# Spectral filter and segmented attention on one core: part of the spectrum's butterflies on GpSimd, and the third bf16 part of q and k by a subtraction

## The chip, the cores and the metric

The kernel runs on one core of a Trainium2 chip. A core has five engines that work side by side, each on its own queue of instructions in a fixed order: TensorE (PE, matrix products), VectorE (DVE), ScalarE (ACT), GpSimd (POOL) and SyncE (SP, which here only issues transfers). They wait for each other by semaphores. The metric is the time of one execution on the device in microseconds (us); lower is better.

## The reference

Two independent computations, side by side in the output. A is a segmented attention with a memory (32 heads of width 18, four segments of 512 rows), B multiplies the 2-D Fourier spectrum of x by a weight.

```python
# A: x (2048 x 576); N = 4 segments of L = 512, H = 32 heads, Dh = 18
q, k, v = x @ wq, x @ wk, x @ wv              # split into heads and segments
for s in range(4):
    logits = einsum("bhqd,bhkd->bhqk", qs, ks) * scale + causal_mask
    a_dot = softmax(logits) @ vs
    a_mem = (phi(qs) @ M) / (phi(qs) . z + 1e-6)      # phi(t) = t+1 if t>0 else exp(t)
    o = g * a_mem + (1 - g) * a_dot                   # g = sigmoid(beta) per head
    M, z = M + phi(ks)^T @ vs, z + sum(phi(ks))
a = concat(o) @ wo
# B: x (2048 x 576)
b = irfft2(rfft2(x) * (w_r + 1j * w_i), s=(2048, 576))
out = concatenate([a, b], axis=-1)
```

## The kernel before

All engines' orders are written out by hand: the order in which the Python program emits instructions is the order of each engine's queue, and nothing reorders them. The time falls into these stages.

1. **Forward transform** (`FFT.forward`, about the first 75 us). For each of 16 units u: VectorE makes sums and differences of two halves of x (`eo`, L125) and low parts (`el`, L131, L132), TensorE multiplies by the tables of the row transform (L142), ScalarE and VectorE split the result in a high and a low part (`X`, L146, L149), TensorE does the 128-point column transform (L162) and ScalarE puts the result in `Z` (L153). `Z` holds 16 complex tiles of 128 x 290 in four by four, real and imaginary parts side by side, so that one tile is 580 elements wide. GpSimd's queue issues the loads of the coefficients `cfw` (L118, four buffers). VectorE also splits the weights wq and wk (L406).
2. **Projections** (`projections`, about 75 to 285 us): four groups g of 512 rows; in each, nine q/k units (14 products of 512 columns, L460, then splitting the result in three bf16 parts that are stored by SP) and four v units (28 products of 288 columns; GpSimd's memsets L507 and L508 fill the constant columns of the v tile, ScalarE copies the values, and the state M, z is accumulated by `pm` (L517), masked by VectorE (L525) and added by GpSimd (L529 to L533)). In the same stage x of the next group is split (L433, L439).
3. **Inverse transform** (`inverse`, about 285 to 355 us) and **attention** (to the end).

The rest of the column transform lies between the first and the third stage: `Z` needs, along its axis of sixteen, a four-point butterfly over each column of tiles (`stage1`), twiddle factors (`tws`, products by a constant on ScalarE and the additions on VectorE), for each c a second butterfly, the product by the weight W, an inverse butterfly and inverse twiddles (`middle`), and a last butterfly (`last`). A butterfly `bf` is ten VectorE instructions (L206): six of 580 elements and four of 290, from `Z` into four temporaries and back to `Z`; there are 16 of them. A weight product is four instructions (L245, L247 of 580 and L250, L252 of 290); there are 16. The tiles of W are loaded by SP (L235, three buffers), each load behind the product that frees its buffer.

These chains are generators that yield after each VectorE instruction, in one list `pace.q`. `Pace.take(f)` lets f of their instructions into the queue at that place. So `forward` takes one per unit from the eighth unit on and two per unit from the fifteenth; `projections` takes w per unit, spread over the four groups, w being 2.4 times as large for a v unit as for a q/k unit.

The splitting of q and k (`qk_unit`) goes: ScalarE writes the first bf16 part from the accumulator in PSUM (L472) and, where needed, computes phi (L475, L476); VectorE finishes phi (L478) and subtracts the first part from the accumulator (L479); ScalarE writes the second part (L483); TensorE subtracts it by a product with the negative identity `nid` (L485), and ScalarE writes the third part (L486). The accumulators are five PSUM buffers.

Of the kernel before, what the change touches and what calls it, by code (L numbers as in the profile page):

```python
# [102 lines left out]
class FFT:  # L103
# [4 lines left out]
    def forward(s,xp,cp,pp,wl,xs,consts):  # L108
# [88 lines left out]
    def bf(s,x,y,inv):  # L197

        v=s.nc.vector; tp=s.tp
        t=[tp.tile([128,2,FP],F32,name=f"t{i}",tag="t",bufs=8) for i in range(4)]  # L200
        p,m=(y[1],y[3]) if not inv else (y[3],y[1])
        for o,a,b,op in ((t[0],x[0],x[2],OP.add),(t[1],x[0],x[2],OP.subtract),(t[2],x[1],x[3],OP.add),(t[3],x[1],x[3],OP.subtract),
                         (y[0],t[0],t[2],OP.add),(y[2],t[0],t[2],OP.subtract),
                         (p[:,0],t[1][:,0],t[3][:,1],OP.add),(p[:,1],t[1][:,1],t[3][:,0],OP.subtract),
                         (m[:,0],t[1][:,0],t[3][:,1],OP.subtract),(m[:,1],t[1][:,1],t[3][:,0],OP.add)):
            v.tensor_tensor(o,a,b,op=op)  # L206
            yield
    def tws(s,L,inv):

        nc=s.nc; v=nc.vector; A=[]; L=[x for x in L if x[1]]  # L210
        if not L: return
        for i in range(len(L)+1):
            if i<len(L):
                y,e=L[i]; a=-2*np.pi*e/16*(-1 if inv else 1)
                t=[s.tp.tile([128,2,FP],F32,name=f"tw{k}",tag="t",bufs=8) for k in range(2)]
                nc.scalar.activation(t[0],y,AF.Copy,scale=float(np.cos(a)))
                nc.scalar.activation(t[1],y,AF.Copy,scale=float(np.sin(a)))
                A.append((y,t))
                if i==0: yield
            if i>0:  # L220
                y,t=A.pop(0)
                v.tensor_tensor(y[:,0],t[0][:,0],t[1][:,1],op=OP.subtract)
                yield
                v.tensor_tensor(y[:,1],t[0][:,1],t[1][:,0],op=OP.add)
                yield
    def stage1(s,b):
        x=[s.Z[:,b,a] for a in range(4)]
        yield from s.bf(x,x,False)
        yield from s.tws([(x[c],b*c) for c in (2,1,3)],False)
    def middle(s,wp):  # L230
        nc,io=s.nc,s.io; v=nc.vector
        Ws=[]
        def ld(i):
            W=wp.tile([128,2,FP],F32,name="W",bufs=3)
            nc.sync.dma_start(W,io["w"][i//4][:,i%4])  # L235
            Ws.append(W)
        for i in range(3): ld(i)
        for c in range(4):
            x=[s.Z[:,b,c] for b in range(4)]
            yield from s.bf(x,x,False)  # L240
            for d in range(4):
                W=Ws[4*c+d]
                t=s.tp.tile([128,2,FP],F32,name="wm",tag="t",bufs=8)
                t2=s.tp.tile([128,2,FP],F32,name="wm2",tag="t",bufs=8)
                v.tensor_tensor(t,x[d],W[:,0][:,None,:].to_broadcast([128,2,FP]),op=OP.mult)  # L245
                yield
                v.tensor_tensor(t2,x[d],W[:,1][:,None,:].to_broadcast([128,2,FP]),op=OP.mult)  # L247
                if 4*c+d+3<16: ld(4*c+d+3)
                yield
                v.tensor_tensor(x[d][:,0],t[:,0],t2[:,1],op=OP.subtract)  # L250
                yield
                v.tensor_tensor(x[d][:,1],t[:,1],t2[:,0],op=OP.add)  # L252
                yield
            yield from s.bf(x,x,True)
            yield from s.tws([(x[b],b*c) for b in (2,1,3)],True)
# [12 lines left out]
    def last(s):  # L268

        for b in range(4):  # L270
            x=[s.Z[:,b,c] for c in range(4)]
            yield from s.bf(x,x,True)
# [69 lines left out]
BF=mybir.dt.bfloat16  # L342
# [42 lines left out]
class ATT:  # L385
# [36 lines left out]
    def xprep(s,g,t,hp,xp,w,tag,bufs):  # L422
# [12 lines left out]
        else:  # L435
            l=s.ftp.tile([128,2,FP],F32R,name="xt",tag="t",bufs=8).rearrange("p a b -> p (a b)")[:,:512]
# [25 lines left out]
    def qk_unit(s,g,mt,tp,pp):  # L462
# [22 lines left out]
        nc.tensor.matmul(ps,s.nid,sp3[:,1],start=False,stop=True,skip_group_check=True)  # L485
        nc.scalar.copy(sp3[:,2],ps)  # L486
# [47 lines left out]
    def projections(s,xp,tp,pp,wv,pace,hook):  # L534

        live=[]
        s.nid=wv.tile([128,128],BF,name="nid"); s.nc.scalar.activation(s.nid,s.ident,AF.Copy,scale=-1.0)
# [505 lines left out]
def emit(nc,tc,io):  # L1043
    def pool(es,name,bufs=1,**kw):
        return es.enter_context(tc.tile_pool(name=name,bufs=bufs,reuse_waits="tile",**kw))
    with ExitStack() as L0:
# [9 lines left out]
        with tc.manual_schedule():  # L1056
# [5 lines left out]
            with ExitStack() as es:  # L1062
                wv=pool(Rv,"wv"); xp=pool(es,"xp"); tp=pool(es,"tp",2); fwp=pool(es,"fw",2)
                pp=es.enter_context(PP(tc,"pp",dict(pj=5,pt=1,pm=2)))
                F.pace.add(F.middle(fwp)); F.pace.add(F.last())
# [13 lines left out]
                A.projections(xp,tp,pp,wv,F.pace,hook)  # L1079
# [37 lines left out]
```

## Time and profile before

| | us |
|---|---|
| median of 3 runs | 725.89 |
| lowest, highest | 725.75, 726.9 |
| span of the profiled execution | 725.3 |
| busy time in that span: TensorE / VectorE / ScalarE / GpSimd | 693.1 / 551.2 / 455.1 / 209.4 |

The profiled execution's own time is its span and lies 0.6 us below the median of the runs. In the rows below, PE is TensorE, DVE VectorE, ACT ScalarE, POOL GpSimd, and SPq the queue of transfers on SyncE. A row of grouped instructions has the line, engine, operation, what is written and read, the shapes and the count, then busy us and mean ns of one, then the engine's idle time before them and who ended it. A row of the timeline has start and duration in us. A row by stretch has, for each engine, busy us and instructions in brackets.

### The profile page before, as it was taken

The page shows a single profiled execution, that of the slowest core. Times are in us where ns is not written, and L with a number is a line of the kernel's source. Part 1 is how long each engine was busy: PE and PEld are TensorE (multiplying, and loading weights), DVE is VectorE, ACT ScalarE, POOL GpSimd, SP SyncE. Part 2 cuts the span into 40 slices and gives each one's busy share as a digit, 9 for nine tenths or more (in the row PEclk, how much of TensorE's full clock was granted, in tenths as well). Part 3 has the DMA queues.
Part 4 walks back from the last instruction along what each step waited for, and adds up shares of the span by engine and source line. Part 5 has one row for each costly group of instructions (what it writes and reads, how often), then busy time and mean ns, then how long its engine had stood idle before and what let it go on. Part 6 is the DMA issues. An engine that isn't in the chain of part 4 may idle for free.

```text
span 725.3 us, 14481 instructions
## 1 busy us (share of the span) xinstructions
PE 693.1 (96%) x5007; PEld 498.8 (69%) x5007; DVE 551.2 (76%) x1281; ACT 455.1 (63%) x1008; POOL 209.4 (29%) x410
## 2 busy tenths in 40 slices
PE   4998999999999999999999999999899999999897
PEld 4988779879779889999844444444565445663397
DVE  6999879899799789787587878877466875667433
ACT  3665796585586574444487777767466776567531
POOL 2111000100200112565065434444142762335310
PEclk9999999999999999999999999999999999999999
DMA  9884435545363668898537656777546675441142
GB/s 339 274 261 156 136 127 183 193 168 177 124 217 131 189 206 275 208 234 224 168 102 185 173 148 146 186 165 159 141 98 172 176 172 133 111 118 41 33 144 84
DMA packets 83245, 121.06 MB, mean 167 GB/s; under 512 B 11352, under 2 KB 50630, under 8 KB 83036
## 3 DMA queue, kind: packets, MB, share of 16 engines
q1 hardware_dynamic: 76580, 104.11, 50.5%
q0 software_dynamic: 6592, 16.03, 7.8%
q8 instruction: 39, 0.64, 0.4%
q14 instruction: 34, 0.28, 0.1%
HBM read 81.78 MB, written 38.24 MB: 165 GB/s over the span
## 4 chain that ended last, share of the span: by engine, by line
PE 76%; DVE 8%; DMA 7%; ACT 5%; issue 3%; POOL 1%; SPq 0%; ACTq 0%; DVEq 0%; POOLq 0%
PE pj L460 14%; PE pv L709 9%; PE s L638 9%; PE pjv L460 8%; PE po L843 7%; PE i L296 4%; PE i L307 4%; PE s L681 3%; PE s L685 2%; PE po L872 2%; DVE eo L125 2%; PE s L690 2%; PE pn L778 2%; PE s L647 2%; PE pm L517 2%
## 5 line engine op out<-in xcount | busy, mean ns | idle before, releaser
L642 DVE CUSTOM_DVE_ANT_0 junk<-s,x 128x512 bf16<-128x512 f32 (+1 forms) x256 | 141.2, 552 | 62.3 <-PE s L638 58.6
L694 POOL TENSOR_SCALAR_AFFINE_SELECT P<-P 128x512 f32<-128x512 f32 x128 | 78.5, 645 | 82.3 <-ACT P L682 74.6
L648 DVE TENSOR_REDUCE mx<-s 128x4 f32<-128x512 f32 x128 | 87.9, 687 | 12.8 <-PE s L647 11.0
L709 PE MATMUL pv<-P,vs 128*32 128x512 f32 (+3 forms) x1024 | 88.8, 442 | 1.0 <-POOL P L694 1.0
L682 ACT ACTIVATE P<-s 128x512 f32<-128x512 f32 x128 | 76.2, 595 | 13.7 <-PE s L681 11.0
L691 ACT ACTIVATE P<-s 128x256 f32<-128x256 f32 x128 | 49.1, 384 | 52.8 <-PE s L690 52.5
L687 ACT ACTIVATE P<-s 128x512 f32<-128x512 f32 x128 | 75.7, 591 | 0.0
L638 PE MATMUL s<-Ks,Qs 108*128 108x384 bf16 (+3 forms) x256 | 69.1, 302 | 1.1 <-DVE mx L648 0.9
L460 PE MATMUL pj<-x,wqkh 128*128 128x512 f32 x162 | 56.5, 409 | 0.0
L638 PEld LDWEIGHTS <-Qs 108*128 108x128 bf16 x320 | 31.6, 99 | 31.5 <-issue 21.9
L206 DVE TENSOR_TENSOR Z<-t,t 128x290 f32<-128x290 f32 (+1 forms) x96 | 48.4, 553 | 0.1
L206 DVE TENSOR_TENSOR t<-Z 128x580 f32<-128x580 f32 x64 | 46.1, 755 | 0.0
L507 POOL MEMSET vt<- 128x32 f32 x16 | 2.3, 161 | 150.5 <-PE pm L517 123.9
L647 PE MATMUL s<-tri,idb 128*128 128x128 bf16 x256 | 43.0, 219 | 0.0
L142 PE MATMUL f<-ftab,eh 128*128 128x290 f32 (+1 forms) x160 | 30.8, 310 | 9.4 <-DMA ftab<-ftab 9.4
L296 PE MATMUL i<-civ,Y 128*128 128x256 f32 (+1 forms) x288 | 39.2, 288 | 0.2 <-POOL Y L281 0.2
L296 PEld LDWEIGHTS i<-civ,Y 128*128 128x128 f32 (+1 forms) x288 | 36.5, 181 | 1.1 <-POOL Y L281 0.4
L709 PEld LDWEIGHTS pv<-P,vs 128*32 128x32 f32 x1024 | 22.1, 108 | 21.9 <-issue 14.5
L307 PE MATMUL i<-itab,T 128*128 128x290 f32 (+1 forms) x224 | 36.3, 305 | 0.1
L460 PE MATMUL pj<-x,wqkl 128*128 128x512 f32 x90 | 35.5, 395 | 0.0
L460 PE MATMUL pj<-xh,wqkl 128*128 128x512 f32 x90 | 35.5, 395 | 0.0
L460 PE MATMUL pj<-xh,wqkh 128*128 128x512 f32 x90 | 35.5, 395 | 0.0
(201 smaller groups left out, 1809.8 us busy)
## 6 DMA issues: line engine op xcount, KB each, us to landing
qkD<-sp SPq DMA_DIRECT2D x36, 384.0 KB
Ks<-qkD SPq DMA_DIRECT2D x72, 144.0 KB
x<-qkD SPq DMA_DIRECT2D x60, 144.0 KB
Qs<-qkD SPq DMA_DIRECT2D x60, 144.0 KB
xin<-xb SPq DMA_DIRECT2D x16, 384.0 KB
cfw<-cfw POOLq DMA_DIRECT2D x16, 384.0 KB, 4.5
civ<-civ POOLq DMA_DIRECT2D x16, 384.0 KB, 7.4
vs<-vD SPq DMA_DIRECT2D x16, 330.0 KB
```

What stands on the lines that cost most here:

```text
L206: v.tensor_tensor(o,a,b,op=op)
L296: nc.tensor.matmul(p[:m,k],Y[i][:,q,c*128:c*128+m],cc[:,hl,o:o+256],start=n==0,stop=n==5)
L307: nc.tensor.matmul(p,x,t,start=n==0,stop=n==6)
L460: s.nc.tensor.matmul(out,a,b,start=i==0,stop=i==len(L)-1)
L638: nc.tensor.matmul(out,Q[:108,h,128*i:128*i+128],K[:108,h,:128*(i+1)],start=True,stop=True)
L642: nc.vector.tensor_tensor_reduce(out=junk[:,:w],in0=src,in1=s.mask[:,512-w:],scale=1.0,scalar=-3.0e38, op0=OP.add,op1=OP.max,accum_out=s.m ...
L647: nc.tensor.matmul(pa[:,o+w-128:o+w],s.idb,s.tri,start=False,stop=True,skip_group_check=True)
L648: nc.vector.tensor_reduce(out=s.mx[k][:,hh],in_=pa.rearrange("p (b c) -> p b c",c=128),axis=mybir.AxisListType.X,op=OP.max)
L682: nc.scalar.activation(P[0][:,hh],p0,AF.Exp,scale=SC)
L687: nc.scalar.activation(P[1][:,hh],p1,AF.Exp,scale=SC)
L694: nc.gpsimd.affine_select(out=x,in_=x,pattern=pat+[[1,128]],compare_op=OP.is_ge,fill=0.0,base=0,channel_multiplier=-1)
L709: nc.tensor.matmul(s.pvt[32*hh:32*hh+32,128*j:],vt[:,j,19*h:19*h+32],mv[0][:,hh,mv[1]],start=j==0,stop=j==2,skip_group_check=True)
```

## The change

- **Butterflies in place.** `bf` works in `Z` itself with two temporaries instead of four: the difference goes to a temporary, the sum over its first operand. The instructions stay ten, six of 580 and four of 290.
- **Part of the chains on GpSimd.** The engine is an argument. GpSimd gets the butterflies of the first stage for b = 0 and 1, and for c = 0 and 1 of the middle both butterflies and the weight products: 20 and 72 instructions. The twiddles stay on ScalarE and VectorE; where a GpSimd chain comes before them they are put at the head of VectorE's list. `s.part` counts finished parts: the middle begins when four are finished, the last butterflies when eight are.
- **Two lists.** `gp` is a second `Pace`. `forward` takes three of its instructions per unit, ahead of the loads of `cfw` in GpSimd's queue; VectorE's list is taken from only after the fourteenth unit. `projections` takes 72/28 of `gp` per unit and w of VectorE's list, now 3.0 times as large for v units.
- **Buffers.** VectorE's temporaries go from eight to five, GpSimd has two of its own, W has two buffers for each of the two chains instead of three in all.
- **Third part of q and k.** The product with `nid` and ScalarE's cast are replaced by one VectorE subtraction from PSUM that writes bf16. `nid` is gone.

```diff
-        s.pace=Pace(61+165+40)
+        s.pace=Pace(41+94+40); s.gp=Pace(20+72); s.part=0
...
-            if u%4==3 and u>6: s.pace.add(s.stage1((u-7)//4))
+            if u%4==3 and u>6:
+                b=(u-7)//4
+                (s.gp if b<2 else s.pace).add(s.stage1(b))
...
-            if u<14: s.pace.take(1)
+            s.gp.take(3)
...
+    def temp(s,eng,n):
+        g=eng is s.nc.gpsimd
+        return [s.tp.tile([128,2,FP],F32,name=f"{'g' if g else 't'}{i}",tag="g" if g else "t",bufs=2 if g else 5) for i in range(n)]
+    def bf(s,x,inv,eng):
+        A,B=s.temp(eng,2)
+        p,m=(x[1],x[3]) if not inv else (x[3],x[1])
+        for o,a,b,op in ((A,x[0],x[2],OP.subtract),(x[0],x[0],x[2],OP.add),(B,x[1],x[3],OP.subtract),(x[1],x[1],x[3],OP.add),
+                         (x[2],x[0],x[1],OP.subtract),(x[0],x[0],x[1],OP.add),
+                         (p[:,0],A[:,0],B[:,1],OP.add),(p[:,1],A[:,1],B[:,0],OP.subtract),
+                         (m[:,0],A[:,0],B[:,1],OP.subtract),(m[:,1],A[:,1],B[:,0],OP.add)):
+            eng.tensor_tensor(o,a,b,op=op)
+            yield
...
     def stage1(s,b):
+        tw=s.tws([(x[c],b*c) for c in (2,1,3)],False)
+        if b<2:
+            yield from s.bf(x,False,s.nc.gpsimd)
+            if b==1: s.pace.q.insert(0,s.count(tw))
+            else: s.part+=1
+        else:
+            yield from s.bf(x,False,s.nc.vector)
+            yield from s.count(tw)
+    def count(s,g):
+        yield from g
+        s.part+=1
-    def middle(s,wp):
+    def middle(s,wp,cs,eng):
+        while s.part<4: yield
...
+            W=wp.tile([128,2,FP],F32,name="Wg" if g else "W",bufs=2)
...
     def last(s):
+        while s.part<8 and s.gp.one(): pass
+        while s.part<8: yield from s.pace.q.pop(0)
...
-        nc.tensor.matmul(ps,s.nid,sp3[:,1],start=False,stop=True,skip_group_check=True)
-        nc.scalar.copy(sp3[:,2],ps)
+        nc.vector.tensor_tensor(sp3[:,2],ps,sp3[:,1],op=OP.subtract)
...
-                w=tot/(36+16*2.4)*(1.0 if i<9 else 2.4)
+                w=tot/(36+16*3.0)*(1.0 if i<9 else 3.0); gw=72/28.0
                 advance()
-                pace.take(w*.4)
+                pace.take(w*.4); gp.take(gw*.4)
                 advance()
                 next(u)
-                pace.take(w*.6)
+                pace.take(w*.6); gp.take(gw*.6)
...
-                F.pace.add(F.middle(fwp)); F.pace.add(F.last())
+                F.gp.add(F.middle(fwp,(0,1),nc.gpsimd)); F.pace.add(F.middle(fwp,(2,3),nc.vector)); F.pace.add(F.last())
```

More of the change, by code (lines that the diff above doesn't have):

```diff
@@ L214, in tws @@
                 y,e=L[i]; a=-2*np.pi*e/16*(-1 if inv else 1)
-                t=[s.tp.tile([128,2,FP],F32,name=f"tw{k}",tag="t",bufs=8) for k in range(2)]
+                t=s.temp(v,2)
                 nc.scalar.activation(t[0],y,AF.Copy,scale=float(np.cos(a)))
@@ L236, in ld @@
+    def count(s,g):
+        yield from g
+        s.part+=1
+    def middle(s,wp,cs,eng):
+        nc,io=s.nc,s.io; g=eng is nc.gpsimd
+        while s.part<4: yield
+        Ws=[]; J=[(c,d) for c in cs for d in range(4)]
+        def ld():
+            if len(Ws)==len(J): return
+            c,d=J[len(Ws)]
+            W=wp.tile([128,2,FP],F32,name="Wg" if g else "W",bufs=2)
+            nc.sync.dma_start(W,io["w"][c][:,d])
             Ws.append(W)
[L237 to L238 removed]
+        ld(); ld()
+        for n,c in enumerate(cs):
@@ L239, in middle @@
             x=[s.Z[:,b,c] for b in range(4)]
-            yield from s.bf(x,x,False)
+            yield from s.bf(x,False,eng)
             for d in range(4):
[L242 to L245, printed above, removed]
+                W=Ws[4*n+d]
+                t,t2=s.temp(eng,2)
+                eng.tensor_tensor(t,x[d],W[:,0][:,None,:].to_broadcast([128,2,FP]),op=OP.mult)
@@ L253, in middle @@
                 yield
-            yield from s.bf(x,x,True)
-            yield from s.tws([(x[b],b*c) for b in (2,1,3)],True)
+            yield from s.bf(x,True,eng)
+            tw=s.tws([(x[b],b*c) for b in (2,1,3)],True)
+            if g and c: s.pace.q.insert(0,s.count(tw))
+            elif g: s.part+=1
+            else: yield from s.count(tw)
     def inv_setup(s,cp):
@@ L533, in v_unit, with projections @@
                 nc.gpsimd.tensor_tensor(z,m[:r,:w,18],s.zst[g][:r,t,:w],op=OP.add)
-    def projections(s,xp,tp,pp,wv,pace,hook):
-        live=[]
-        s.nid=wv.tile([128,128],BF,name="nid"); s.nc.scalar.activation(s.nid,s.ident,AF.Copy,scale=-1.0)
+    def projections(s,xp,tp,pp,wv,F,hook):
+        live=[]; pace,gp=F.pace,F.gp
         lw=s.load_w("wv",576,wv,xp,288,"xl",4)
@@ L1078, in emit @@
                 q0=[]
-                A.projections(xp,tp,pp,wv,F.pace,hook)
+                A.projections(xp,tp,pp,wv,F,hook)
             Rv.close()
```

28 lines of the change are left out of this document (6 added, 22 removed).

## The prediction

> **What bounds the kernel now.** I read the page first (busy shares, chain), then busy times by stage, then the rows of VectorE and GpSimd in the stages that the change touches.
>
> ```profile
> span 725.3 us, 14481 instructions
> ...
> PE 693.1 (96%) x5007; PEld 498.8 (69%) x5007; DVE 551.2 (76%) x1281; ACT 455.1 (63%) x1008; POOL 209.4 (29%) x410
> ...
> PE 76%; DVE 8%; DMA 7%; ACT 5%; issue 3%; POOL 1%; SPq 0%; ACTq 0%; DVEq 0%; POOLq 0%
> ```
>
> TensorE is busy nearly throughout, but the shares are means over stages. By stretch (16.5 us of the forward transform, then the four groups of the projections):
>
> ```profile
> core 0: us, PE busy (x) PEld busy (x) DVE busy (x) ACT busy (x) POOL busy (x), PEclk, DMA share, GB/s
> 42.00:58.50 16.50, 15.09 (x105) 14.15 (x106) 16.25 (x29) 10.23 (x21) 2.12 (x4) 1.00 0.82 248
> 75.56:127.98 52.42, 51.22 (x289) 43.13 (x288) 44.91 (x89) 41.78 (x85) 0.35 (x4) 1.00 0.47 155
> 127.98:180.94 52.96, 52.96 (x308) 45.16 (x308) 48.11 (x89) 34.39 (x67) 3.06 (x18) 1.00 0.57 184
> 180.94:235.00 54.06, 53.50 (x308) 45.44 (x308) 45.78 (x86) 37.91 (x74) 4.30 (x18) 1.00 0.46 158
> ```
>
> In the forward transform VectorE is the bound (16.25 of 16.5 us). In the projections TensorE is, with VectorE at 85 to 91%. GpSimd is nearly idle in both, which is where the change puts its work. From about 285 us on (inverse, attention) the change touches nothing and I take it as shifted only.
>
> **Part 1: the product.** Its price on TensorE is the step between projection tiles:
>
> ```profile
> 245.56 3.26 PE pj L460 x14
> 249.04 3.26 PE pj L460 x14
> ```
> ```profile
> L485 PE MATMUL pj<-sp,nid x36: 376/389/393, 83.6 to 273.9; 128*128 128x512 bf16 x36
> ```
>
> One tile is 3.26 us and the next starts 3.48 us later: 0.22 to 0.23 us per product, so 36 x 0.23 = 8.3 us where TensorE stays the bound, about 2.05 us for each group of nine. ScalarE loses 36 casts that stood behind it. VectorE gains 36 subtractions from PSUM, which I price by the row of the same shape:
>
> ```profile
> L478 DVE SCALAR_TENSOR_TENSOR ex<-pj,ex 128x512 f32<-128x512 f32 x9 | 6.2, 689 | 5.1 <-ACT ex L476 4.9
> L479 DVE TENSOR_TENSOR pj<-pj,sp 128x512 f32<-128x512 f32 x9 | 6.2, 689 | 0.0
> L206 DVE TENSOR_TENSOR Z<-t,t 128x290 f32<-128x290 f32 x12 | 4.9, 453 | 0.0
> L206 DVE TENSOR_TENSOR Z<-t,t 128x580 f32<-128x580 f32 x6 | 4.4, 752 | 0.0
> ...
> L433 DVE TENSOR_TENSOR xl<-xst,xh 128x512 fp32r<-128x512 f32 x4 | 2.7, 684 | 0.0
> ```
> ```profile
> 46.66 1.02 DVE L125 TENSOR_TENSOR eo<-xin 128x384 f32<-128x384 f32 x2
> 47.60 0.76 DVE L149 TENSOR_TENSOR X<-f,X 128x580 fp32r<-128x580 f32 x1
> 48.27 0.75 DVE L206 TENSOR_TENSOR t<-Z 128x580 f32<-128x580 f32 x1
> 48.94 0.68 DVE L131 TENSOR_TENSOR el<-eo,eh 128x512 fp32r<-128x512 f32 x1
> 49.66 0.42 DVE L132 TENSOR_TENSOR eh<-eo,eh 33x256 fp32r<-33x256 f32 x1
> 50.11 0.76 DVE L406 TENSOR_TENSOR wqkl<-raw,wqkh 128x576 fp32r<-128x576 f32 x1
> ```
>
> Starts lie 0.08 us closer than durations (47.60 to 48.27 is 0.67 for 0.75), so a VectorE step is 0.67 us for 580 wide, 0.61 for 512, 0.37 for 290. The new subtraction adds 36 x 0.61 = 22 us to VectorE.
>
> **Part 2: what GpSimd takes.** A butterfly is 6 instructions of 580 and 4 of 290; a weight product 2 and 2. GpSimd gets 2 butterflies in the forward transform (20 instructions) and 4 butterflies with 8 products in the projections (72). For VectorE that is 6 x 5.5 + 8 x 2.08 = 50 us less. GpSimd's own rates:
>
> ```profile
> L813 POOL TENSOR_TENSOR ol<-am,oh 126x512 fp32r<-126x512 f32 x8 | 10.2, 1273 | 8.6 <-ACT oh L810 6.8 <-PE s L690 1.7
> ...
> L610 POOL TENSOR_TENSOR wol<-ob,woh 126x576 fp32r<-126x576 f32 x5 | 7.1, 1411 | 7.0 <-ACT woh L609 6.5 <-PE s L686 0.5
> ...
> L739 POOL TENSOR_TENSOR ry<-ry,rw 128x128 f32<-128x128 f32 x8 | 3.4, 429 | 23.0 <-ACT rw L738 22.9
> ```
>
> A line through 128, 512 and 576 gives 0.15 us + 2.19 ns per element: 1.42 us at 580, 0.79 at 290. 92 instructions are 105 us, twice what VectorE takes.
>
> **Do they run side by side?** The trace has a few places where both engines read two operands from SBUF:
>
> ```profile
> 700.03 0.43 POOL L739 TENSOR_TENSOR ry<-ry,rw 128x128 f32<-128x128 f32 x1 [14.48 <-ACT rw L738]
> 700.53 0.63 POOL L740 CAST rw<-ry 128x128 bf16<-128x128 f32 x1
> 701.24 0.75 POOL L741 TENSOR_TENSOR rw<-ry,rw 128x128 bf16<-128x128 f32 x1
> ```
> ```profile
> 700.13 0.88 DVE L854 TENSOR_TENSOR ux<-ux,am 126x512 f32<-126x512 f32 x1
> 700.93 0.77 DVE L859 TENSOR_TENSOR P<-ux,P 126x512 fp32r<-126x512 f32 x1
> 701.63 0.68 DVE L853 TENSOR_TENSOR ux<-ux,pb 126x512 f32<-126x512 f32 x1
> 702.34 0.69 DVE L854 TENSOR_TENSOR ux<-ux,am 126x512 f32<-126x512 f32 x1
> ```
>
> L854 takes 0.88 us behind L739 and 0.69 alone: it ends 0.55 us after L739's end, so it stood until 0.14 us before that end. L741, of L739's shape, takes 0.75 instead of 0.43: it ends 0.29 us after L859, again 0.14 before the end of the other. L740 got in between L854 and L859, so the engines take turns. L853, which reads one operand from PSUM, runs beside L741 at its usual 0.68. So a two-SBUF-operand instruction of one engine holds off the other's for its duration less 0.14 us, and only VectorE's PSUM instructions cover GpSimd. Hold times: GpSimd 1.28 (580) and 0.645 (290), VectorE 0.61 and 0.31. A butterfly on GpSimd holds 10.3 us, a product 3.85: 20.5 us in the forward transform, 71.8 in the projections.
>
> The Trainium skill (SBUF — State Buffer, Who interferes with whom) has the two engines' shared pair as a lock held for the whole instruction. By that, each of the 92 would hold 0.14 us longer, 13 us in all; the rows above show the release earlier, and I sum by the rows.
>
> **Forward transform.** One iteration on VectorE is 4.13 us, all of it taken. Without its butterfly instruction it is 3.46, with X (0.67, from PSUM) as the only cover. GpSimd is handed three instructions per iteration, 3.08 us of hold. Over 6.7 iterations VectorE then has 23.1 + 20.5 us less an overlap of at most 4.5 (X), 39.1 against 27.5 before: +11.6; without any overlap +16. If GpSimd falls behind into the last, emptier iterations, less is paid: +3. GpSimd's queue also issues the coefficient loads (cfw) behind these instructions; they are used three iterations later, so a lag of some 8 us stays hidden. I take +9.
>
> **Projections.** VectorE's pace falls to 153/84 = 1.82 instructions per q/k unit and 5.46 per v unit, 38 per group; GpSimd's middle part starts when the first stage is complete (third v unit of the first group) and runs 28 units at 2.57: 2.15 groups. In such a group VectorE's own steps are 27 PSUM instructions (16.5 us), the state products (1.2), five x splits (3.0), 38 spectrum instructions at 0.51 (19.6) and some 1.4 us of waits on its own earlier instruction, which chains in place have more often: 41.7 us. TensorE needs 54.06 - 2.05 = 52.0. GpSimd holds 33.4 x 1.0 = 33.3 us. For the group to stay at 52.0, 23.0 of these 33.3 must fall on VectorE's PSUM instructions and idle time (28 us together). Holds alone (20.1 + 33.3) give 53.4 us as the least; an overlap of half the PSUM time gives 66. I take 17 us of overlap: 58, since a q/k unit has 2 or 3 PSUM instructions in a row against one 1.28 us hold. That is +4 per group against 54.06, x 2.15 = +8.6 [-1.5 to +26]. The other 1.85 groups gain 2.05 each: -3.8. The loads of weights on SP's queue:
>
> ```profile
> SPq L235 <- DVE wm L247: 28.6, 13, 4.6
> ```
>
> They go from three buffers to two per chain, and half of them then wait for a GpSimd product, with the stores of q, k and v queued behind. I price it at 0 while the q/k tiles are three buffers deep; it costs up to this row's 4.6 us a time where that cover is used up. The ring of temporaries (8 to 5) costs nothing: a butterfly in place needs two of them instead of four.
>
> **Sum**: 725.3 (the profiled execution, 0.6 below the median) + 9 + 8.6 - 3.8 = 739.1; against the median of 725.89 that is **739.7**.
>
> **Rivals.**
> A, faster: the cover suffices. VectorE has 10.3 us idle per group plus 17.7 of PSUM work; if GpSimd fills 23 of it and lags harmlessly in the forward transform, TensorE stays the bound: 725.9 - 8.3 + 3 = 720.5 (down to 717.6 with no loss at all). Point of decision: 23 us of overlap per group. For it: GpSimd's idle; against: holds of 1.28 us are longer than two PSUM steps. Chance 0.20.
> B, worse: GpSimd's order becomes the bound.
>
> ```profile
> POOL vt L507 <- DMA vD<-vt: 16.6, 3, 8.5
> ...
> DVE mm L525 <- POOL zst L533: 2.1, 6, 0.5
> ```
>
> Memsets of v tiles wait up to 8.5 us for a store, with butterflies now queued behind; ScalarE's v copies wait for those memsets, and VectorE's state products for GpSimd's copies, behind its whole backlog. A lag of 5 to 8 us at three group ends: 739.7 + 15 to 24, about 757. Chance 0.15.
> C, the hold lasts for whole instructions under load: up to 13 us more, 750. The same page of the Trainium skill says this; chance 0.03.
> D, gains and losses cancel within 0.2% (which is what a measurement tells from no change): 0.04.
>
> Forecast (734 to 750): 0.58. With C that makes slower 0.76, same 0.04, faster 0.20. The range 720 to 758 takes in most of A and B.
>
> **What would show it.** Right: VectorE's 580-wide SBUF instructions rise from 0.75 to over 1.2 us on average beside GpSimd's, those from PSUM stay at 0.69; the forward iterations go from 4.1 to 5 us or more; TensorE is idle in the second and third group; L485 is gone. Wrong: if durations stay at 0.75 under load, or TensorE stays dense from 120 to 230 us, A holds; if GpSimd is idle behind memsets while ScalarE waits for them, B.

## The result, and the profile after

The changed kernel takes 754.3 us (median; 752.5 to 754.8) against 725.8 for the kernel before in the same rounds: ratio 1.039 [1.037, 1.041], slower by 28.5 us. The forecast was slower by 13.8 in a range of 720 to 758. The page of the changed kernel, its span, busy shares, granted clock in 40 slices, and shares of the chain that ended last:

```profile
span 752.1 us, 14427 instructions
...
PE 692.3 (92%) x4971; PEld 503.5 (67%) x4971; DVE 584.5 (78%) x1225; ACT 436.6 (58%) x971; POOL 323.0 (43%) x502
...
PEclk9988999999999999999999999999999999999999
...
PE 60%; DVE 19%; ACT 7%; issue 6%; DMA 4%; POOL 3%; SPq 0%; DVEq 0%; ACTq 0%; POOLq 0%
```

TensorE has no more work than before (692 against 693 us) and VectorE has 56 instructions fewer, yet VectorE is busy for 33 us longer: its instructions have become longer. The chain runs through VectorE for 19% of the span instead of 8. By stage, from the starts of the first projection product and the first inverse product in each trace:

| stage | before | after | difference | forecast |
|---|---|---|---|---|
| forward transform, to the first projection | 75.4 | 94.0 | +18.6 | +9 |
| projections | 208.0 | 217.7 | +9.7 | +4.8 |
| inverse and attention | 441.9 | 440.4 | -1.5 | 0 |
| span | 725.3 | 752.1 | +26.8 | +13.8 |

Stage times here and below come from one profiled execution of each kernel. How far they can be trusted shows in the seven kernels below whose forward transform is VectorE's alone: it ends between 74.6 and 76.8 us, so a difference of 1 or 2 us in a stage proves little.

The busy times by stretch: first the same seven forward iterations (from the sixth `X` to the thirteenth) in the kernel before and in the changed kernel, where GpSimd's butterflies fall into them; then the four groups of the projections in the changed kernel (52.4, 53.0, 54.1 and 48.6 us before). Columns as in the prediction.

```profile
core 0: us, PE busy (x) PEld busy (x) DVE busy (x) ACT busy (x) POOL busy (x), PEclk, DMA share, GB/s
31.40:60.84 29.44, 27.58 (x192) 25.94 (x192) 28.69 (x51) 17.88 (x35) 4.03 (x8) 1.00 0.79 242
```
```profile
31.84:78.12 46.28, 31.70 (x200) 29.98 (x199) 43.82 (x44) 17.86 (x35) 28.73 (x28) 0.85 0.53 161
94.00:142.80 48.80, 48.80 (x281) 42.65 (x280) 44.99 (x75) 33.81 (x69) 7.80 (x9) 1.00 0.54 170
142.80:204.70 61.90, 54.48 (x301) 47.42 (x300) 60.23 (x78) 31.61 (x61) 44.16 (x53) 0.94 0.47 159
204.70:265.30 60.60, 52.89 (x300) 45.91 (x300) 58.33 (x73) 30.14 (x59) 45.95 (x52) 0.97 0.42 141
265.30:311.67 46.37, 46.37 (x259) 40.67 (x259) 38.83 (x73) 25.23 (x50) 6.61 (x22) 1.00 0.73 238
```

The first group, with five of GpSimd's spectrum instructions, and the last, with none (7.8 and 6.6 us busy), got shorter, by 3.6 and 2.2 us, with TensorE busy to the last tenth. The two with GpSimd at 44 to 46 us got longer, by 8.9 and 6.5, and there VectorE has only 1.7 and 2.3 us left idle, with 73 to 78 instructions against 86 to 89 before. In the forward iterations VectorE is busy for 43.8 of 46.3 us with 44 instructions, 1.00 us each; before it was 51 in 28.7, 0.56 each.

Which instructions got longer, in the second group of the changed kernel (grouped by line and form: busy us, mean ns of one, idle before):

```profile
L210 DVE TENSOR_TENSOR Z<-Z 128x580 f32<-128x580 f32 x8 | 10.6, 1324 | 0.2
L454 DVE TENSOR_TENSOR x<-xst,x 128x512 fp32r<-128x512 f32 x4 | 6.2, 1558 | 0.0
L261 DVE TENSOR_TENSOR t<-Z,W 128x580 f32<-128x580 f32 x4 | 6.2, 1549 | 0.0
L500 DVE TENSOR_TENSOR pj<-pj,sp 128x512 f32<-128x512 f32 x9 | 6.1, 683 | 0.0
L506 DVE TENSOR_TENSOR sp<-pj,sp 128x512 bf16<-128x512 f32 x9 | 6.1, 678 | 0.0
L499 DVE SCALAR_TENSOR_TENSOR ex<-pj,ex 128x512 f32<-128x512 f32 x9 | 6.1, 677 | 0.3 <-ACT ex L497 0.3
```

The split is clean. Instructions with both operands in SBUF take 1.3 to 1.6 us instead of 0.75 (580) or 0.68 (512). Instructions that read one operand from PSUM, the new L506 among them, keep their 0.68. GpSimd pays too, though less: 1.72 us for an instruction of 580 over both groups, against 1.42 on the prediction's line.

```profile
L210 POOL TENSOR_TENSOR Z<-Z 128x580 f32<-128x580 f32 x16 | 27.4, 1715 | 0.8
```

One figure is used from here on, the **stretch**: the sum over VectorE's instructions of their duration less the short (5th per cent) duration of the same form, where that is over 0.06 us. It is worked out from all rows of VectorE's timeline. Beside it stands what VectorE was **relieved** of, at the prediction's 5.5 us per butterfly and 2.08 per weight product, and GpSimd's hold times as the prediction added them up.

| | relieved | hold | stretch |
|---|---|---|---|
| before, projections | 0 | 0 | 0.1 |
| after, forward transform | 11.0 | 20.5 | 18.7 |
| after, projections | 38.6 | 71.8 | 42.0 |

In both stages VectorE loses more by standing than it was relieved of: 60.7 us against 49.6. The holds are a little high: the prediction's line gave 0.79 us at 290, where the shortest in the changed kernel is 0.69 to 0.70, and the shortest of the weight product's 580 is 1.32. With these the holds are 19.8 and 67.5 us, and the stretch is 94 and 62% of them instead of 91 and 58%.

### The profile page after: what moved, and what is told of

It reads as the page before. It is cut to its first block, busy times and chain, and to the rows that moved or that the text cites. A ratio compares the mean times of both kernels' runs of the same rounds, so it can differ in the third digit from the quotient of the medians.

```text
span 752.1 us, 14427 instructions
## 1 busy us (share of the span) xinstructions
PE 692.3 (92%) x4971; PEld 503.5 (67%) x4971; DVE 584.5 (78%) x1225; ACT 436.6 (58%) x971; POOL 323.0 (43%) x502
## 3 DMA queue, kind: packets, MB, share of 16 engines
q1 hardware_dynamic: 76580, 104.11, 48.6%
## 4 chain that ended last, share of the span: by engine, by line
PE 60%; DVE 19%; ACT 7%; issue 6%; DMA 4%; POOL 3%; SPq 0%; DVEq 0%; ACTq 0%; POOLq 0%
PE pv L728 9%; PE s L657 9%; PE po L862 7%; PE pj L481 6%; PE pjv L481 5%; PE i L317 4%; PE i L328 4%; PE s L700 3%; DVE Z L210 2%; DVE eo L125 2%; PE s L704 2%; PE po L891 2%; DVE wqkl L427 2%; PE s L709 2%; PE s L666 2%
## 5 line engine op out<-in xcount | busy, mean ns | idle before, releaser
L710 ACT ACTIVATE P<-s 128x256 f32<-128x256 f32 x128 | 49.1, 383 | 52.9 <-PE s L709 52.5
L504 ACT CAST sp<-pj 128x512 bf16<-128x512 f32 x36 | 21.1, 585 | 57.8 <-DVE pj L500 57.8
L162 PE MATMUL c<-X,cfw 128*128 128x290 f32 x192 | 32.1, 322 | 19.6 <-ACT Z L153 19.5
L162 PEld LDWEIGHTS c<-X,cfw 128*128 128x128 f32 x192 | 28.9, 207 | 21.9 <-ACT Z L153 21.9
L210 POOL TENSOR_TENSOR Z<-Z 128x580 f32<-128x580 f32 x24 | 40.3, 1678 | 1.3
L682 POOL CAST mh<-mg 128x16 bf16<-128x16 f32 x32 | 6.2, 194 | 78.3 <-ACT mg L680 47.1
L210 DVE TENSOR_TENSOR Z<-Z 128x580 f32<-128x580 f32 x40 | 38.7, 966 | 1.0
```

The lines of the kernel that those rows point to most:

```text
L162: nc.tensor.matmul(p[:,:FP],cc[:,hl,k*128:(k+1)*128],x[i][:,q],start=n==0,stop=n==5)
L210: eng.tensor_tensor(o,a,b,op=op)
```

## The experiments

The theory: GpSimd's two-operand instructions and VectorE's from SBUF exclude each other, and what VectorE stands there is the loss. The rival: VectorE has no room for the 36 subtractions of part 1, whatever GpSimd does. Most runs below take one of them away or leave one alone. The butterflies in place and the shorter rings of buffers were not run by themselves; the memset run below has both and is the fastest of all, so the loss isn't theirs. Ratios are against the kernel before, timed in the same rounds.

### The subtractions alone

```diff
 (kernel before)
-        nc.tensor.matmul(ps,s.nid,sp3[:,1],start=False,stop=True,skip_group_check=True)
-        nc.scalar.copy(sp3[:,2],ps)
+        nc.vector.tensor_tensor(sp3[:,2],ps,sp3[:,1],op=OP.subtract)
```

> The subtraction alone: the kernel before with the product by nid and ScalarE's cast replaced by VectorE's subtraction, everything of the spectrum left on VectorE as before. Port theory (GpSimd's two-operand instructions hold off VectorE's): nothing on GpSimd, so only part 1 remains: TensorE loses 36 x 0.23 = 8.3 us, VectorE gains 5.5 us in a group of 54 us where it had 8.3 idle, so it just fits: 718 to 724 us. Rival (VectorE is already too full, and the 22 us of subtractions are a good part of the loss): 727 to 735 us.

Measured: 737.5 us, ratio 1.016 [1.013, 1.019]. Slower, above both expectations: part 1 alone costs 11.7 us. Its four groups and the beginning of the inverse transform:

```profile
75.90:127.30 51.40, 49.20 (x280) 42.52 (x279) 49.02 (x95) 37.63 (x75) 0.34 (x4) 1.00 0.48 157
127.30:179.80 52.50, 51.41 (x300) 44.59 (x299) 50.24 (x92) 27.76 (x54) 2.89 (x16) 1.00 0.57 185
179.80:237.80 58.00, 52.10 (x301) 44.63 (x300) 54.33 (x103) 35.38 (x68) 4.47 (x20) 1.00 0.44 148
237.80:284.20 46.40, 46.40 (x260) 40.68 (x259) 41.86 (x78) 23.46 (x47) 6.61 (x22) 1.00 0.72 237
284.20:300.00 15.80, 9.35 (x58) 8.74 (x57) 13.49 (x21) 5.52 (x14) 5.68 (x8) 0.80 0.41 122
```

VectorE goes to 94 to 96% in the first three groups. They save 1.0 and 0.5 us instead of 2.05 each, and the third loses 3.9. The projections take as long as before (208.3 against 208.0 us), but less of the spectrum is done by then: 24 of VectorE's spectrum instructions start behind the first inverse product, against 17 before, and the inverse transform takes 82.7 us against 74.0. They meet a second thing there, GpSimd's subtractions for Y:

```profile
288.67 2.37 POOL L281 TENSOR_TENSOR Y<-Z,Y 128x512 fp32r<-128x512 f32 x2 [1.98 <-ACT Y L280]
290.54 4.36 DVE L206 TENSOR_TENSOR Z<-t,t 128x580 f32<-128x580 f32 x5
295.60 4.18 PE L296 MATMUL i<-civ,Y 128*128 128x256 f32 x18 [5.46 <-issue]
```

Five instructions of 580 take 4.36 us in which they would take some 3.4 alone (0.67 each), and TensorE stands for 5.46 us before its next products (the profile names no releaser, so that VectorE's lateness is what it waits for is not shown). So the rival is real: VectorE's room is gone with 22 us more.

### GpSimd's part alone

```diff
 (changed kernel)
-        nc.vector.tensor_tensor(sp3[:,2],ps,sp3[:,1],op=OP.subtract)
+        nc.tensor.matmul(ps,s.nid,sp3[:,1],start=False,stop=True,skip_group_check=True)
+        nc.scalar.copy(sp3[:,2],ps)
```

> The GpSimd chains alone: the changed kernel with the product by nid and ScalarE's cast put back. If the loss is the GpSimd chains' alone and the product's 8.3 us come on top: 758 to 763 us. If VectorE is the bound in the groups with GpSimd, the 5.5 us of subtractions per group that it loses are worth more there than TensorE's 2 us, and cost 2 us each in the other two: 745 to 753 us. The forward transform is not touched: it ends at 93 to 95 us by either.

Measured: 753.7 us, ratio 1.037 [1.033, 1.041], just above the second expectation, and the changed kernel's time: beside GpSimd's chains, part 1 neither gains nor loses. The groups say how:

```profile
94.77:146.20 51.43, 51.15 (x290) 43.07 (x288) 41.39 (x68) 38.55 (x79) 7.80 (x9) 1.00 0.50 163
146.20:202.60 56.40, 53.58 (x310) 45.40 (x308) 54.47 (x67) 36.10 (x70) 45.22 (x52) 1.00 0.50 173
202.60:265.40 62.80, 55.63 (x310) 47.07 (x308) 58.54 (x69) 36.07 (x70) 46.96 (x53) 0.97 0.40 136
265.40:313.89 48.49, 48.49 (x269) 41.11 (x268) 31.75 (x59) 28.39 (x57) 6.62 (x22) 1.00 0.70 229
```

Against these the changed kernel is 2.6 and 2.1 us shorter in the first and last group, where TensorE is the bound: the price of nine products, as the prediction had it. In the two groups with GpSimd it is 5.5 longer and 2.2 shorter. Even without the subtractions those two groups last 56.4 and 62.8 us with VectorE at 93 to 97% and only 67 to 69 instructions, so GpSimd's part alone makes VectorE the bound. The stretch is 19.1 us in the forward transform and 46.0 in the projections.

### GpSimd's instructions without their reads

GpSimd's 92 instructions become groups of memsets of two or three each, so that they last about as long. The spectrum's values are left out by this, since the sums and products that GpSimd had are not computed.

```diff
+    def fill(s,o,w=None):
+        for i in range(3 if len(o.shape)==3 else 2): s.nc.gpsimd.memset(w if w is not None and i==0 else o,0.0)
...
-            eng.tensor_tensor(o,a,b,op=op)
+            if eng is s.nc.gpsimd: s.fill(o)
+            else: eng.tensor_tensor(o,a,b,op=op)
 (and in the same way at the four instructions of the weight product)
```

> The changed kernel with each of GpSimd's 92 two-operand spectrum instructions replaced by memsets (three where 580 elements are written, two where 290) into the same tiles, so that GpSimd is as long busy, in the same order with the same waits, but reads nothing from SBUF; the spectrum's values are left out. Port theory: VectorE's instructions go back to 0.75 us at 580 wide, the forward transform ends at 72 to 76 us instead of 94, and the time is 714 to 722 us. Rival (GpSimd's queue is late, and the memsets, state copies and loads behind it are what stalls the rest): as late as before, 742 to 756 us.

Measured: 716.2 us, ratio 0.986 [0.984, 0.989], as the theory had it. Second and third group, and VectorE's butterfly instructions of 580 in the second:

```profile
124.40:175.30 50.90, 50.90 (x300) 44.76 (x299) 40.26 (x73) 31.73 (x61) 41.66 (x103) 1.00 0.57 194
175.30:226.30 51.00, 51.00 (x301) 44.87 (x300) 41.16 (x76) 31.62 (x61) 43.60 (x105) 1.00 0.50 168
```
```profile
L213 DVE TENSOR_TENSOR Z<-Z 128x580 f32<-128x580 f32 x6 | 4.6, 758 | 0.1
```

GpSimd is as busy as in the changed kernel (42 to 44 us a group), its order and buffers are the same, and the subtractions are there; its reads of two operands are gone. VectorE is back at 0.76 us for 580 wide and at 40 to 41 us a group, TensorE is busy without a gap, the forward transform ends at 75.7 us, and the groups last 51 us. The 38 us between this run and the changed kernel hang on those reads. The Trainium skill (SBUF — State Buffer, Who interferes with whom) has a VectorE instruction with two SBUF inputs contend with a GpSimd instruction that reads SBUF and not with one that only writes it; the 758 ns here and the 1324 above agree.

### GpSimd in one stage only

```diff
 (changed kernel; first: GpSimd only in the middle)
-        if b<2:
+        if b<0:
 (stage1's four butterflies all go to VectorE's list, with one per unit from the eighth unit on as before)
 (second: GpSimd only in the forward transform)
-                F.gp.add(F.middle(fwp,(0,1),nc.gpsimd)); F.pace.add(F.middle(fwp,(2,3),nc.vector)); F.pace.add(F.last())
+                F.pace.add(F.middle(fwp,(0,1,2,3),nc.vector)); F.pace.add(F.last())
```

> The changed kernel with the two first-stage butterflies back on VectorE, one instruction per forward unit as in the kernel before; GpSimd keeps its 72 instructions in the projections. Port theory: the forward transform ends near 75.6 us as before (the changed kernel 94.2), the groups with GpSimd stay at 60 to 62 us: 733 to 739 us. Rival (the stages are not separable, a late forward transform hides part of the projections' loss): 740 to 748 us.

> The changed kernel with the whole middle on VectorE; GpSimd keeps only the 20 first-stage instructions. Port theory: forward transform ends near 94 us as in the changed kernel (+18.6), projections as in the subtraction alone: its time + 18, 734 to 744 us. Rival (VectorE too full with subtractions and the whole middle): 745 us or more.

Measured: 746.9 us, ratio 1.029 [1.026, 1.032], for the middle only, and 753.2, 1.038 [1.035, 1.041], for the forward transform only. Both lie in the ranges given for the rival. For the second that says little: the theory's range was the time of the subtractions alone plus 18, and these took 737.5 us instead of the 718 to 724 that it was set up with.

With the middle only, the forward transform ends at 74.6 us, so that its whole loss is GpSimd's butterflies. The two groups with most of GpSimd's work take 59.7 and 62.4 us, about as expected. The projections as a whole take 225.0 us, 7.3 more than in the changed kernel, and that lies in the first group (52.0 us against 48.8, with 81 VectorE instructions against 74) and in the last (50.9 against 46.4), into which GpSimd's work now reaches. The stretch is the same (41.4 us). So the stages are not separable, as the rival had it. Against the run with the subtractions alone, this kernel differs by the 72 instructions on GpSimd: 38.6 us taken off VectorE, 41.4 of stretch put on, 9.4 us slower.

With the forward transform only, that stage ends at 92.5 us (stretch 17.5), the projections take 210.4 and the inverse transform 83.1: the loss of the forward transform plus about that of the subtractions alone (+17.1, +2.4, +9.1, where the subtractions alone had +0.3 in the projections and +8.7 in the inverse transform).

### GpSimd's forward instructions spread out

```diff
 (changed kernel)
-            s.gp.take(3)
+            s.gp.take(1.5)
```

> The changed kernel with 1.5 of GpSimd's instructions per forward unit instead of 3, so that its 20 spread over 13 units, the last five of which leave VectorE little to do. If every microsecond that GpSimd holds the port is lost to VectorE wherever it falls: the forward transform still ends at 91 to 95 us, and the time stays within 751 to 757 us. If it is the bursts (six 580-wide instructions in a row, one VectorE instruction let in between two of them, while TensorE runs dry): the end moves to 82 to 88 us and the time to 742 to 749 us.

Measured: 751.3 us, ratio 1.036 [1.033, 1.039], at the lower edge of the first expectation, while the end of the forward transform, 87.8 us, is at the upper edge of the second. Neither is met as a whole. In the profiled execution (746.3 us) the seven iterations that had 46.3 us take 39.1, and the whole forward transform still has 16.7 us of stretch:

```profile
32.58:71.71 39.13, 31.30 (x207) 29.89 (x205) 36.67 (x44) 17.91 (x35) 19.68 (x20) 0.91 0.67 199
```

Only 12 of GpSimd's 20 instructions fall into these iterations. Of their 12.8 us of hold 11.5 came back as stretch, 90%, so spacing doesn't make VectorE and GpSimd overlap. The other eight start from 77 us on, where VectorE has room: from 71.7 us to the first projection it has 10 us of its own work in 16, and that time is as long as in the changed kernel (16.1 us against 15.9). What spacing gives back, 6.3 us of the forward transform, is hold moved to where it costs little. The projections then take 3.3 us more (220.9 against 217.7); no run shows why.

### GpSimd only beside VectorE's instructions from PSUM

If only VectorE's PSUM instructions cover GpSimd, then GpSimd should be let go just then. Here GpSimd has one first butterfly of the middle (c = 0) and its four products, 26 instructions, one of 580 or two of 290 per q/k unit, each behind a one-element copy that reads VectorE's last output from two SBUF operands. The rest is on VectorE; the subtractions stay.

```diff
 (changed kernel)
+    def gslot(s):
+        try: ops=next(s.gops)
+        except StopIteration: return
+        if not ops: return
+        g=s.nc.gpsimd; l=s.lastv
+        if l is not None:
+            l=l[:,0] if len(l.shape)==3 else l
+            g.tensor_copy(s.gscr,l[:,:1])
+        for o,a,b,op in ops: g.tensor_tensor(o,a,b,op=op)
...
-                pace.take(w*.4); gp.take(gw*.4)
+                pace.take(w*.4)
+                if i<11: F.gslot()
```

> The changed kernel's subtraction, the first stage on VectorE, and of the middle only the first butterfly and the four weight products of c = 0 on GpSimd (26 instructions): one of 580 or two of 290 per q/k unit, released by a copy of one element that VectorE's last two-SBUF instruction before its three PSUM instructions (1.8 us in a row) has written. Port theory: GpSimd's 1.28 us of hold lie beside PSUM instructions and cost VectorE next to nothing, VectorE's two-SBUF instructions stay near 0.75 us at 580 in the groups, VectorE has 14 us less than in the subtraction alone (737.5): 717 to 726 us. Rival (VectorE is late all the same, it does not run its PSUM instructions when GpSimd is released): 732 to 742 us.

A companion leaves out the copy, so that GpSimd's instructions start when they can:

```diff
-            g.tensor_copy(s.gscr,l[:,:1])
+            pass
```

> The kernel with 26 GpSimd instructions beside PSUM instructions (v2), without the one-element copy that releases each of them: the same instructions in the same order, but each runs as soon as GpSimd is free. If it is the timing against VectorE's PSUM instructions that decides: the time by which VectorE's instructions are longer than alone rises from 3.9 us to 10 to 16 us (0.4 to 0.6 of 25.7 us of hold, as in the changed kernel's projections), and the time to 742 to 752 us against 739.4. If fewer GpSimd instructions alone made it small: 3 to 6 us and 737 to 741 us.

Measured: 739.4 us, ratio 1.019 [1.016, 1.022], with the copy; 746.3, 1.027 [1.025, 1.029], without. The first misses the theory's time (717 to 726) and lies in the rival's range, though VectorE's instructions did stay short; the second is as the theory had it. The same 26 instructions, the same work, 0.8% of the time apart. VectorE's groups of 580, with the copy and then without:

```profile
L210 DVE TENSOR_TENSOR Z<-Z 128x580 f32<-128x580 f32 x44 | 33.8, 769 | 1.2
L294 DVE TENSOR_TENSOR t<-Z,W 128x580 f32<-128x580 f32 x12 | 9.1, 754 | 0.3 <-DMA W<-w 0.2
L296 DVE TENSOR_TENSOR t<-Z,W 128x580 f32<-128x580 f32 x12 | 9.8, 817 | 0.0
```
```profile
L210 DVE TENSOR_TENSOR Z<-Z 128x580 f32<-128x580 f32 x38 | 31.1, 819 | 0.9
L294 DVE TENSOR_TENSOR t<-Z,W 128x580 f32<-128x580 f32 x12 | 11.3, 945 | 0.2
L296 DVE TENSOR_TENSOR t<-Z,W 128x580 f32<-128x580 f32 x12 | 11.8, 987 | 0.0
```

With the copy the stretch is 3.9 us of 25.7 us of hold, without it 14.0. So GpSimd's work can be hidden when it is placed behind VectorE's last SBUF instruction; left to itself, more than half of it isn't. The time still isn't under the kernel before: only 13.8 us are relieved this way, less than the 22 of the subtractions. As with the subtractions alone, the loss comes late: the inverse transform takes 83.0 us against 74.0, and 25 of VectorE's spectrum instructions start behind its first product. VectorE is at 86 and 94% in the first two groups; the first, in which GpSimd has nothing to do yet, is 2.4 us longer than before, and no run shows why:

```profile
76.00:130.80 54.80, 51.01 (x281) 43.70 (x280) 47.12 (x89) 37.53 (x75) 0.34 (x4) 0.97 0.43 142
130.80:186.30 55.50, 52.79 (x299) 46.16 (x299) 51.98 (x92) 31.59 (x61) 22.68 (x43) 0.97 0.53 176
```

### Fewer subtractions

Three tries for a version that beats the kernel before. First, the subtractions in the first two groups alone, with no GpSimd:

```diff
 (kernel before)
+        if g<2:
+            nc.vector.tensor_tensor(sp3[:,2],ps,sp3[:,1],op=OP.subtract)
+        else:
             nc.tensor.matmul(ps,s.nid,sp3[:,1],start=False,stop=True,skip_group_check=True)
             nc.scalar.copy(sp3[:,2],ps)
```

> The kernel before with the subtraction in the first two of the four groups only, the product kept in the others. In the subtraction alone these two groups took 51.4 and 52.5 us against 52.4 and 53.0 before, and the loss came in the third (58.0 against 54.0) and in the inverse transform (82.7 against 74.0). If each group pays for itself: 722 to 725.5 us. Rival: what VectorE is late in the first two groups is paid in the next, 727 to 733 us.

Measured: 726.2 us, ratio 0.999 [0.997, 1.002]: no difference, and between the two ranges. The first three groups take 51.4, 52.5 and 56.7 us against 52.4, 53.0 and 54.1: half of the subtractions fit, and what TensorE saves in the first two groups is paid in the third.

Then the released GpSimd chain with the subtractions in the second and third group, and that with VectorE's list shared out by 0.9, 1.1, 1.15 and 0.85 over the groups:

```diff
 (kernel with GpSimd beside the PSUM instructions)
+        if g in (1,2):
             nc.vector.tensor_tensor(sp3[:,2],ps,sp3[:,1],op=OP.subtract)
+        else:
+            nc.tensor.matmul(ps,s.nid,sp3[:,1],start=False,stop=True,skip_group_check=True)
+            nc.scalar.copy(sp3[:,2],ps)
...
-                w=tot/(36+16*3.0)*(1.0 if i<9 else 3.0); gw=72/28.0
+                w=tot/(36+16*2.4)*(1.0 if i<9 else 2.4)
 (masks of the attention: built at i==12 of the last group, not at i==3; `nid` is made in the tile of `idb`)
 (the second of the two: w also times (0.9,1.1,1.15,0.85)[g])
```

> v2 with the subtraction in the second and third group only, where GpSimd takes VectorE's work, and the product (with ScalarE's cast) kept in the first and last; v units' share of the pace 2.4 as in the kernel before. VectorE gains 11 us of subtractions and 4 us of held-off time and loses 14 us: about even with the kernel before, and TensorE has 18 x 0.23 = 4.1 us less: 721 to 724 us. Rival (VectorE at this load makes TensorE wait wherever the two meet): 726 to 732 us.

> v3 with VectorE's pace weighted by 0.9, 1.1, 1.15 and 0.85 over the four groups, so that the last butterflies come earlier. If lateness at the start of the inverse transform is what is left: 1 to 3 us faster than v3. If the second and third group are as full as the others: 1 to 4 us slower than v3.

Measured: 730.0 us, ratio 1.004 [1.003, 1.006], and 736.3, 1.015 [1.012, 1.017]. The first lies in the rival's range; the second is slower than the first by 6 us, more than either expectation had. The stretch is small in both (3.1 and 5.2 us), so it isn't what limits them; that it is VectorE's load in the groups with subtractions is likely (in the first of the two the second group takes 57.1 us against 53.0) but not shown. No version here that computes the whole result is faster than the kernel before.

## Why the prediction was right and wrong

**What held.** The mechanism and its signs. VectorE's SBUF instructions of 580 rose over 1.2 us beside GpSimd's (1324 and 1549 ns), those from PSUM stayed at 0.68, the forward iterations went over 5 us (46.3 / 7 = 6.6), TensorE had gaps in the second and third group alone, and L485 is gone. The memset run shows that the shared reads carry the whole loss. What failed is the size of two terms, and with it the sum: +28.5 us is twice +13.8. That 754.3 still lies in the range of 720 to 758 is luck in part, since the upper end was put there for B, which isn't what happened.

**The step that failed first: the forward term, "I take +9". Measured +18.6.** Two things in it were wrong.

The first is the overlap. Without any, the sum was +16; +9 takes 7 us off for X as a cover and for GpSimd falling behind into the emptier iterations. Of 20.5 us of hold 18.7 became stretch, so the overlap was 1.8 us. GpSimd didn't fall behind: the last of its 20 instructions ends at 77.3 us, and VectorE is busy without a break of over 0.3 us up to 83 us. And X meets GpSimd's instructions only three times (at 42.16, 52.29 and 66.38 us). GpSimd's queue holds the load issues too, which wait for the column product to free a buffer, so that it works in bursts and stands between them. VectorE and GpSimd in the changed kernel's timeline:

```profile
36.92 1.87 DVE L427 TENSOR_TENSOR wqkl<-raw,wqkh 128x576 fp32r<-128x576 f32 x1
38.72 3.53 DVE L125 TENSOR_TENSOR eo<-xin 128x384 f32<-128x384 f32 x2
42.16 0.75 DVE L149 TENSOR_TENSOR X<-f,X 128x580 fp32r<-128x580 f32 x1
43.19 0.88 DVE L131 TENSOR_TENSOR el<-eo,eh 128x512 fp32r<-128x512 f32 x1 [0.28 <-ACT eh L127]
```
```profile
38.72 4.80 POOL L210 TENSOR_TENSOR Z<-Z 128x580 f32<-128x580 f32 x3
48.20 0.57 POOL L118 DMA_DIRECT2D cfw<-cfw  x1 [4.68 <-PE c L162]
48.79 2.01 POOL L210 TENSOR_TENSOR Z<-g,g 128x290 f32<-128x290 f32 x3
```

The burst of 38.72 to 43.52 falls on the two sums of halves (1.02 us alone, 3.53 here), and X, the only cover, passes in 0.75. Behind it GpSimd stands for 4.68 us for the buffer. The bursts alone don't explain it: at half the rate 90% of the hold was paid in these iterations, too.

The second is the iteration itself. The prediction took 4.13 less one step, 3.46 us, for an iteration without its butterfly instruction. One that GpSimd doesn't stretch takes 3.82 in the changed kernel (from 51.35 to 55.17 us), and the kernel before has one, just ahead of its first butterfly instruction, of 3.83:

```profile
30.46 1.02 DVE L125 TENSOR_TENSOR eo<-xin 128x384 f32<-128x384 f32 x2
32.44 0.69 DVE L131 TENSOR_TENSOR el<-eo,eh 128x512 fp32r<-128x512 f32 x1 [0.28 <-ACT eh L127]
34.29 1.02 DVE L125 TENSOR_TENSOR eo<-xin 128x384 f32<-128x384 f32 x2
```

With the instruction gone that stood between X and `el`, `el` waits 0.28 us for ScalarE's `eh`, whether GpSimd is at work or not. With 3.82 the prediction's own sum is 6.7 x 3.82 + 18.7 = 44.3 us against 27.5, +16.8, and the seven iterations have grown by 16.8 (46.3 against 29.4). Most of what is left of the +18.6 lies behind them (+1.3), where X waits for ScalarE twice, 1.6 us together. From the view of waits between 30 and 90 us:

```profile
DVE el L131 <- ACT eh L127: 2.3, 8, 0.3
DVE X L149 <- ACT X L146: 1.6, 2, 1.0
```

**The other step, the group with GpSimd, "17 us of overlap: 58": measured 61.9 and 60.6.** In the trace these groups have 41.2 and 40.3 us of VectorE's own work, 19.1 and 18.1 of stretch, and 1.7 and 2.3 of idle time. By the prediction's hold times GpSimd held 33.4 and 32.1 us in them, so the overlap was 14 us instead of 17. The 41.7 for VectorE's own work, with 1.4 us of waits in it, was about 1 too small. So the guess of 17 was 3 too large: the two or three PSUM instructions in a row cover a hold only where it happens to start with them. The companion pair (3.9 against 14.0 us of stretch) shows that this is a matter of when GpSimd's instruction starts.

**"The other 1.85 groups -2.05 each": measured -3.6 and -2.2.** Right in sign and nearly in size; the run with the product put back shows -2.6 and -2.1 for the product itself. The projections in sum: +15.5 in two groups where +8.6 was forecast, -5.8 in the other two where it was -3.8, so that a part of the first error cancels.

**Part 1's 22 us** were counted inside VectorE's 41.7 and that held; but the prediction spoke of TensorE's 2.05 us as the gain wherever it is the bound and didn't say what part 1 would be alone. It is +11.7 us alone and nothing beside GpSimd's chains: the room that GpSimd was to make for it is smaller than the stretch that GpSimd brings.

**The rivals.** A needed 23 us of overlap per group and lost: 14. B, GpSimd's order as the bound, is not it: the memset run has the same order and as busy a GpSimd and takes 716.2 us. In the changed kernel, between 85 and 315 us, VectorE's waits for GpSimd's copies are as short as before, and GpSimd's memsets wait little longer for the stores of v than before (16.6 us):

```profile
POOL vt L527 <- DMA vD<-vt: 20.1, 3, 9.1
...
DVE mm L545 <- POOL zst L553: 2.1, 6, 0.5
```

C, a hold that lasts for whole instructions, was priced at 750 and comes near in time, but not by its mechanism: the stretch of 18.7 us is below the 20.5 that the shorter hold allows, so nothing asks for a longer one, and the last section has the release measured again.

## What to carry to other kernels

Before work goes to GpSimd to relieve VectorE, set the hold (GpSimd's duration of each instruction that reads two operands from SBUF) against what VectorE saves: here 105 us of GpSimd's instructions stood for 49.6 of VectorE's, and 58 to 91% of the hold came back as longer VectorE instructions. Little of it came back (15%) only where GpSimd was made to wait for VectorE's last SBUF instruction and ran beside work that reads PSUM, and writes without reads cost nothing. An engine at 85 to 91% has no room for 22 us more over the stage, even where its idle time, added up, is larger: look at which work of its list then lands in the next stage.

## What the runs showed of the hardware

**Turns are not kept.** The prediction read from the trace that the engines take turns. They do where each of GpSimd's instructions waits for a semaphore first (six of 580 from 33.30 to 43.52 us, with one of VectorE's between two); but three GpSimd instructions of 290 in a row with no wait between them (48.79 above, 2.01 us) kept VectorE out for all three:

```profile
48.39 3.04 DVE L427 TENSOR_TENSOR wqkl<-raw,wqkh 128x576 fp32r<-128x576 f32 x1
51.35 1.02 DVE L125 TENSOR_TENSOR eo<-xin 128x384 f32<-128x384 f32 x2
```

L427 takes 0.76 us alone. It ended at 51.43, 0.63 us after the last of the three (50.80): again 0.13 us less than its own duration, the release of the prediction's rows. Why it stood from 48.39, 0.4 us ahead of GpSimd's first, isn't settled; GpSimd's load issue at 48.20 was then under way. The Trainium skill (SBUF — State Buffer, Who interferes with whom) says that issue order decides who blocks. By the recorded starts VectorE's instruction came first here and stood all the same, so these rows don't agree, or the recorded start isn't the moment that decides; no run here tells which.

**TensorE's clock drops behind VectorE's stalls.** The granted clock over the seven forward iterations is 0.85 (1.00 in the kernel before). The twelve column products after a gap of 6.34 us take 3.27 us, against 1.77 to 1.89 behind shorter gaps in the same trace (the one other gap of over 6 us gives 3.27 too):

```profile
44.63 3.27 PE L162 MATMUL c<-X,cfw 128*128 128x290 f32 x12 [6.34 <-ACT Z L153]
```

So such a stall costs 1.4 us more than itself where these products are next on the path. The Trainium skill (TensorE: Matmul & The Clock Gate, Part 1) has the clock fall after an idle window of some 3.4 us. The two gaps here, 6.3 us, are longer than that, and the products behind one of 3.00 us took 1.88, so the trace agrees. The run with GpSimd's instructions spread out comes closer to it: behind gaps of 3.68 and 3.73 us the same products took 3.27 and 2.37.
